# A fused attention and ELU kernel: the hand-fixed order of all five engines replaced by another one

## The chip, the cores and the metric

The kernel runs on one core of a Trainium2 chip. The metric is the time of one execution on the device in microseconds (us). Before the change three runs gave 298.71 us in the median (298.64 to 298.76). A profile was taken of one further execution, which took 298.42 us; its recorded span, from the first to the last instruction of the program, is 296.2 us. Engines are named as in the profile: PE is the matrix engine (PEld its weight loads), DVE the vector engine, ACT the scalar engine, POOL is GpSimd, SP the engine that only issues DMAs here.

## The reference

```python
q_s = exp(q - max(q, -1));  q_s /= sum(q_s, -1)        # softmax over the 64 features
k_s = exp(k - max(k, 2));   k_s /= sum(k_s, 2)         # softmax over the 576 positions
kv  = einsum('bhsd,bhse->bhde', k_s, v)                # batch 8, heads 8, seq 576, dim 64
a   = einsum('bhsd,bhde->bhse', q_s, kv)
x   = a.transpose(0, 2, 1, 3).reshape(4608, 512)
h   = x @ w_in                                         # 512 -> 2048
g   = where(h > 0, h, exp(min(h, 0)) - 1)
out = g @ w_out                                        # 2048 -> 512, float32
```

## The kernel before

**Two pipelines in one.** The attention part works in 16 units n (a batch's four heads each, n = 0 to 15). The feed-forward part works on 9 blocks j of 512 tokens, each in 8 groups g of 256 hidden features. While the feed-forward part works on block j, the attention units that later blocks need are fed in between.

**Attention unit n.** Loads of q, k, v (`load`, L345; on POOL's DMA queue for the early units, on SP's for the later). `stage1`: ACT takes exponentials of q (L380, for units 0 and 1 in halves, L410) and of k (L384); POOL or ACT turns v to bf16 (L400, L397); DVE sums q's exponentials (L412), takes reciprocals (L415); POOL (for units 0 to 3 POOL and DVE) multiplies them in (L423, result QS). QS is transposed on PE (`tp`, L447, copied out by ACT or DVE, L454 and L457) or, from unit 4 on, by a DMA on SP (`turn`, L463) and widened to fp32r by POOL or ACT (`widen`, L473 and L475). PE makes kv (L503), DVE normalizes it (`m`, L512 and L516), PE multiplies by q (L534, L546), and ACT or DVE copies the result to the ring XT (`xt`, L568 and L571).

**Feed-forward block j, group g.** `hg`: eight matmuls of 128x512 (L619) into one of two pairs of PSUM banks; ACT takes exp (L635). From there one of two ways. Way "a": ACT makes relu(1 - e) (L655) and DVE one or two operations max(h, 0) - that (L658). Way "d" (half of the groups of blocks 0 and 1): DVE makes min(e, 1) - 1 in SBUF (L663) and then the max with h (L665). The next matmuls of that bank pair wait for DVE.

**The second product.** For blocks 0 and 1 it is plain (`out_mm`, L680). For later blocks a seven-product scheme for 2x2 blocks of matrices saves matmuls: `pair` (L874, L880) for half of the features, `whole` (L804) for all. It needs differences of blocks of W2 (`combos`, POOL, L739) and, for every token half (ts) and feature half (hi) of a block, four sums of blocks of g (`sums`, L770), on POOL except for the very last set, which DVE makes. DVE and ACT put the parts together (L894, L810, L906, L922, L815), and SP stores (L713).

**What sets the order.** Every call of `S.add` makes one operation: an engine, a modelled duration, the code that emits it, and what it reads and writes. Operations are numbered as they are made, 0 to 1110. The table `ORDER` lists, for each engine, the numbers of its operations in the order in which that engine gets them. `Sched.order` reads this table, gives each operation a modelled start time, and merges the five lists by it; `fill` puts a few warming matmuls on PE in the modelled gaps of the first microseconds (L969); `emit` writes the instructions and a semaphore wait for each input made by another engine or a DMA. On the chip each engine goes through its own list strictly in order: an operation whose input is late holds up all that stand behind it on the same engine. The modelled durations in the kernel are not used for anything else.

Operations that the text names, by number:

| numbers | engine | what |
| --- | --- | --- |
| 14 to 21 | POOL queue | loads of W1: 14 to 17 groups 0 to 2 by quarters, 18, 19, 20 groups 3, 4, 5 (512 KB each), 21 groups 6 and 7 (1 MB) |
| 110, 121, 133 | PE | L619, block 0, groups 5, 6, 7 |
| 163, 224 | POOL queue, ACT | load of q and L380 for unit 5 |
| 225, 226, 227 | DVE, DVE, POOL | L412, L415, L423 for unit 5 |
| 253, 259, 266, 272, 279 | PE | L619, block 1, groups 2 to 6 |
| 254, 255, 256 | ACT, DVE, DVE | L635, L663, L665 of block 1, group 2 |
| 177, 185 | PE, ACT | last quarter of L680 of block 0 for one token tile, and its copy out (L698) |
| 1046, 1047, 1048, 1049, 1050 | PE, ACT, ACT, DVE, DVE | the last group (block 8, group 7): L619, L635, L655, L658 twice; 1042 is the second L658 of group 6 |
| 1063 to 1066 | DVE | L770, the last set of sums, in the order in which they are made |
| 1055 to 1058, 1062 | POOL | L770, the set before it, and the last of another one |
| 1067 to 1107 | PE | L804, the last block's seven-product pieces |
| 1082, 1083, 1085, 1089, 1090 | DVE | L810, putting the last block together |

Of the kernel before, what the change touches and what calls it, by code (L numbers as in the profile page):

```python
# [23 lines left out]
ISSUE = {"sp": 550, "act": 550, "gp": 740}  # L24
ORDER = {
# [14 lines left out]
    "act": (  # L40
# [12 lines left out]
    "dve": (  # L53
# [30 lines left out]
}  # L84


# [1094 lines left out]
```

## Time and profile before

| | |
| --- | --- |
| median of three runs | 298.71 us |
| the profiled execution | 298.42 us, span 296.2 us |
| busy, of the span | PE 284.3 us (96%), ACT 211.3 (71%), POOL 193.3 (65%), DVE 182.2 (62%) |
| chain that ended last | PE 89%, DVE 5%, ACT 3%, DMA 1%, issue 1% |
| DMA | 36.70 MB read, 9.44 MB written |

The page gives, for each engine, busy time and its share of the span, the chain of work that ended last, and groups of instructions by source line with their mean duration and the idle time ahead of them. The list of waits adds up who waited for whom. The timeline shows instructions in order of time: start, length, engine, line, operation, tiles and shapes, and in brackets the idle time ahead of it and what ended it. Since the program's instructions stand in the trace in the order of `ORDER`, each operation's number can be matched to its instruction, and its start and end read off; the landing of a DMA is read from the update of its semaphore.

### The profile page before, as it was taken

How to read it: one execution, taken by the hardware profiler on the slowest of the kernel's cores; microseconds unless marked ns; L12 is line 12 of the kernel's file. 1: busy time of each engine (PE TensorE's matmuls, PEld its weight loads, DVE VectorE, ACT ScalarE, POOL GpSimd, SP SyncE). 2: the span in 40 equal slices, each digit the busy share in tenths (PEclk: the TensorE clock that was granted, in tenths of full speed). 3: DMA queues.
4: the chain of work that ended last, by engine and by line, in shares of the span. 5: the costliest groups of instructions: out<-in, count | busy, mean ns of one | idle time of the engine just before them, and what ended most of it. 6: DMA issues, size and time to landing. Idle time of an engine off the chain costs nothing.

```text
span 296.2 us, 5181 instructions
## 1 busy us (share of the span) xinstructions
PE 284.3 (96%) x2082; PEld 240.9 (81%) x2082; DVE 182.2 (62%) x327; ACT 211.3 (71%) x249; POOL 193.3 (65%) x155
## 2 busy tenths in 40 slices
PE   2999999989999999999999999999999999999984
PEld 0588877678888888888888888888889998988984
DVE  2858645777663858665766575653544645375793
ACT  4868659968998968888967796776564666566610
POOL 1990347615499993849565657368678976859580
PEclk9999999999999999999999999999999999999998
DMA  7999999898794659389398613122020302021205
GB/s 268 398 364 388 389 390 353 236 234 288 210 276 151 161 139 340 69 242 326 85 204 221 218 36 78 40 55 53 18 55 0 73 18 53 20 53 37 62 11 142
DMA packets 36471, 50.01 MB, mean 169 GB/s; under 512 B 16352, under 2 KB 18144, under 8 KB 36448
## 3 DMA queue, kind: packets, MB, share of 16 engines
q1 hardware_dynamic: 29760, 34.09, 41.6%
q0 software_dynamic: 6528, 15.47, 17.1%
q8 instruction: 16, 0.26, 0.4%
q10 hardware_dynamic: 160, 0.13, 0.2%
q14 instruction: 7, 0.06, 0.1%
HBM read 36.70 MB, written 9.44 MB: 156 GB/s over the span
## 4 chain that ended last, share of the span: by engine, by line
PE 89%; DVE 5%; ACT 3%; DMA 1%; issue 1%
PE PS L619 43%; PE PS L804 11%; PE PS L880 10%; PE PS L680 9%; PE PS L874 9%; PE PS L534 3%; PE PS L503 2%; PE PS L969 2%; DMA QR<-in_q_dram 1%; DVE XT L770 1%; ACT ESB L635 1%; DVE GR L658 1%; DVE ESB L663 1%; PE PS L447 1%; DVE GR L665 1%; ACT ESB L655 1%
## 5 line engine op out<-in xcount | busy, mean ns | idle before, releaser
L619 PE MATMUL PS<-XT,W 128*128 128x512 f32 x576 | 142.6, 393 | 1.6 <-DVE GR L665 1.6
L619 PEld LDWEIGHTS PS<-XT,W 128*128 128x128 f32 x576 | 105.2, 188 | 22.8 <-DVE GR L665 1.7
L658 DVE SCALAR_TENSOR_TENSOR GR<-PS,ESB 128x512 fp32r<-128x512 f32 (+1 forms) x124 | 87.3, 706 | 58.4 <-ACT ESB L655 56.7
L635 ACT ACTIVATE ESB<-PS 128x1024 f32<-128x1024 f32 x72 | 73.7, 1026 | 41.0 <-PE PS L619 40.6
L655 ACT ACTIVATE ESB<-ESB 128x1024 f32<-128x1024 f32 x64 | 67.9, 1061 | 1.6
L423 POOL TENSOR_TENSOR QS<-QR,RZQ 128x1152 f16<-128x1152 f32 (+1 forms) x16 | 30.6, 1913 | 37.5 <-DVE RZQ L415 37.3
L770 POOL TENSOR_TENSOR SB<-GR 128x512 fp32r<-128x512 f32 x18 | 23.3, 1296 | 40.7 <-DVE GR L658 20.7
L880 PE MATMUL PS<-W,GR 128*128 128x512 f32 x128 | 33.1, 392 | 0.0
L680 PE MATMUL PS<-W,GR 128*128 128x512 f32 x128 | 32.3, 395 | 0.0
L680 PEld LDWEIGHTS PS<-W,GR 128*128 128x128 f32 x128 | 23.4, 188 | 4.7 <-DVE GR L665 0.2
L880 PEld LDWEIGHTS PS<-W,GR 128*128 128x128 f32 x128 | 22.7, 189 | 3.8
L412 DVE TENSOR_REDUCE ZQ<-QR 128x18 f32<-128x1152 f32 (+2 forms) x18 | 21.8, 1209 | 6.3 <-ACT QR L410 4.4
L770 POOL TENSOR_TENSOR GR<-GR 128x512 fp32r<-128x512 f32 x19 | 25.4, 1343 | 0.0
L770 POOL TENSOR_TENSOR SB<-GR,SB 128x512 fp32r<-128x512 f32 x18 | 23.7, 1314 | 0.6
L770 POOL TENSOR_TENSOR SB<-SB,GR 128x512 fp32r<-128x512 f32 x18 | 23.7, 1316 | 0.5
L568 ACT ACTIVATE XT<-PS 128x512 fp32r<-128x512 f32 (+6 forms) x32 | 19.2, 604 | 6.3 <-PE PS L534 3.0
L400 POOL CAST VB<-VR 128x1152 bf16<-128x1152 f32 (+1 forms) x16 | 17.7, 1108 | 6.3 <-DMA VR<-in_v_dram 6.3
L894 DVE TENSOR_TENSOR OSB<-OSB,PS 128x256 f32<-128x256 f32 x32 | 13.2, 413 | 12.7 <-PE PS L880 6.3
L384 ACT ACTIVATE KR<-KR 128x1152 bf16<-128x1152 f32 x16 | 18.4, 1154 | 0.5 <-DMA KR<-in_k_dram 0.5
L380 ACT ACTIVATE QR<-QR 128x1152 f32<-128x1152 f32 x14 | 16.2, 1159 | 1.3 <-DMA QR<-in_q_dram 1.3
L804 PE MATMUL PS<-W,GR 128*128 128x256 f32 x96 | 14.1, 283 | 0.0
L804 PE MATMUL PS<-TB,GR 128*128 128x256 f32 x96 | 13.5, 285 | 0.6 <-DVE OSB L810 0.6
(80 smaller groups left out, 335.4 us busy)
## 6 DMA issues: line engine op xcount, KB each, us to landing
out_dram<-OSB SPq DMA_DIRECT2D x60, 128.0 KB, 2.4
QR<-in_q_dram SPq DMA_DIRECT2D x12, 576.0 KB, 5.3
KR<-in_k_dram SPq DMA_DIRECT2D x12, 576.0 KB, 5.3
VR<-in_v_dram SPq DMA_DIRECT2D x12, 576.0 KB, 5.5
W<-in_moe_w_out_dram POOLq DMA_DIRECT2D x4, 1024.0 KB, 16.5
QR<-in_q_dram POOLq DMA_DIRECT2D x4, 576.0 KB, 10.9
KR<-in_k_dram POOLq DMA_DIRECT2D x4, 576.0 KB, 11.0
VR<-in_v_dram POOLq DMA_DIRECT2D x4, 576.0 KB, 13.2
```

Source lines behind the costliest of these rows:

```text
L412: S.add("dve", t_dve(m), lambda e, qp=qp, zp=zp: e.tensor_reduce(zp, qp, AX.X, ALU.add), key - 3, R=[f"qR{i}{x}" for x in xs], W=[f"ZQ{i}{ ...
L423: lambda e, qp=q[:, :, a:b, :], rz=rz, dst=qs[:, :, a:b, :]: e.tensor_tensor(dst, qp, rz, ALU.mult),
L568: S.add("act", t_act((h1 - h0) * n_, True), lambda e, dst=dst, src=src: e.activation(dst, src, AF.Copy), key, W=W, X=X)
L619: last = e.matmul(P[:, t * 512:(t + 1) * 512], self.W1[:, kc, tt * 128:(tt + 1) * 128], self.XT[:, kc, rc:rc + BLK], start=(kc == 0), stop ...
L635: S.add("act", t_act(1024, True), lambda e: e.activation(esb[:, :], self.PS[ps][:, :], AF.Exp), key, W=[f"E{i}"], X=banks)
L655: S.add("act", t_act(1024, False), lambda e: e.activation(esb[:, :], esb[:, :], AF.Relu, bias=1.0, scale=-1.0), key, X=[f"E{i}"])
L658: S.add("dve", t_dve(512 if j else 1024), lambda e, u=u: e.scalar_tensor_tensor(*(x[:, :, u, :] if j else x for x in (gt, P)), 0.0, ev[:, ...
L680: last = e.matmul(dst, self.tile(jb, jj, ts), self.W2[:, jj, c0:c1], start=(jj == 0), stop=(jj == 15))
L770: lambda e, dst=dst, a=a, b=b, op=op: e.tensor_tensor(dst, a, b, op), key, R=R, W=W, X=X,
L804: last = e.matmul(dst, a[:, z, :], b[:, z, :], start=start and z == 0, stop=stop and z == NSP - 1, skip_group_check=True)
L874: last = e.matmul(dst, a[:, z, :], b[:, z, :], start=start and z == 0, stop=stop and z == NSP - 1, skip_group_check=True)
L880: last = e.matmul(self.bank((b0, b1)[p]), self.tile(j, jj, 2 * ts + p), self.W2[:, jj, :], start=False, stop=jj == 15, skip_group_check=True)
```

## The change

The table `ORDER` is replaced by another order of the same 1111 operations. The new order was solved for with a model in which VectorE's operations last longer when they run beside GpSimd's. The operations, their code, their durations in the kernel's own model, tiles and buffers are the same; the numbers of the waits and where the merged list puts them follow from the order. Cut to the parts that the text speaks of ("..." marks what is left out):

```diff
     "pe": (
-        "35 54 33 37 52 57 56 60 78 81 64 65 79 82 84 87 85 88 80 83 86 89 99 103 110 121 133 107 "
-        "148 147 150 155 158 156 125 149 157 127 171 145 170 169 151 176 177 153 168 175 159 178 "
-        "172 165 192 194 191 193 253 259 257 258 264 265 211 266 272 270 271 278 220 279 284 222 "
+        "35 54 33 37 52 56 57 60 78 79 82 64 65 81 80 84 87 85 88 83 86 89 99 103 110 121 107 133 "
+        "148 147 149 150 156 125 157 158 127 155 171 168 169 145 175 176 153 151 170 159 178 172 "
+        "165 192 194 191 177 193 253 259 258 257 264 265 211 266 272 220 271 278 270 279 222 277 "
...
-        "1022 953 980 973 990 987 982 1011 998 1003 1031 1017 1067 1006 1026 1043 1024 1038 1034 "
-        "1046 1069 1051 1070 1072 1071 1073 1068 1077 1075 1088 1081 1084 1079 1095 1091 1098 "
+        "1022 953 973 980 987 982 990 1003 998 1011 1031 1017 1006 1026 1024 1043 1038 1034 1046 "
+        "1067 1051 1070 1069 1072 1068 1073 1071 1077 1075 1081 1084 1079 1088 1095 1091 1098 "
         "1103 1107 "),
     "act": (
...
-        "109 135 115 126 137 146 152 182 138 185 154 179 198 173 166 188 224 249 250 195 207 199 "
-        "254 260 261 210 297 267 273 274 221 280 223 230 286 232 287 236 293 294 233 308 348 240 "
+        "135 115 109 126 137 146 138 182 152 154 179 198 173 166 188 224 249 250 185 195 199 207 "
+        "254 260 261 210 297 267 273 274 221 233 280 223 230 286 232 287 236 293 294 348 308 334 "
...
     "dve": (
...
-        "225 226 251 252 196 197 255 256 262 263 212 213 214 215 216 217 268 269 275 276 298 299 "
+        "225 251 252 196 197 255 226 256 262 263 212 213 214 215 216 217 268 269 275 276 298 281 "
...
-        "1001 1002 1032 1033 1020 1007 1021 1029 1030 1035 1044 1045 1041 1042 1052 1049 1050 "
-        "1063 1064 1065 1089 1066 1082 1083 1085 1090 1096 1097 1092 1099 1100 1104 1108 "),
+        "1001 1002 1032 1033 1020 1021 1029 1030 1007 1044 1035 1045 1041 1052 1049 1050 1042 "
+        "1063 1064 1082 1083 1066 1065 1085 1089 1090 1096 1097 1092 1099 1100 1104 1108 "),
     "gp": (
-        "1 32 48 14 15 24 16 17 18 40 19 20 21 68 69 70 71 72 74 73 75 76 77 120 131 116 144 143 "
-        "163 132 139 164 200 205 203 208 227 234 300 237 386 303 311 318 387 388 390 314 321 391 "
+        "1 32 48 14 15 24 17 16 18 40 19 21 20 68 69 70 71 72 73 74 75 76 77 120 116 131 144 143 "
+        "163 139 164 132 200 205 203 208 227 234 300 237 386 303 311 318 387 388 390 391 314 321 "
...
-        "867 873 896 874 897 898 915 916 917 899 969 972 970 971 962 963 964 965 918 994 997 995 "
-        "1013 1059 1060 1014 996 1061 1015 1016 1055 1056 1057 1058 1062 "),
+        "866 896 873 897 874 898 915 916 917 969 899 970 971 918 962 963 965 964 994 995 972 996 "
+        "1013 1016 997 1059 1060 1014 1061 1015 1062 1055 1056 1057 1058 "),
     "sp": (
-        "8 9 10 11 12 13 184 186 190 204 206 209 189 180 228 183 219 218 235 181 229 187 301 238 "
+        "8 9 10 11 12 13 180 204 206 187 183 209 218 181 228 229 219 184 186 235 189 190 301 302 "
...
```

72 rows, old and new, of the table ORDER are left out of this document.

## The prediction

> **What bounds the kernel now.** I read the page's first part and its chain first, then the waits of PE alone, then the timeline at the two places where those waits fall.
>
> ```profile
> span 296.2 us, 5181 instructions
> PE 284.3 (96%) x2082; PEld 240.9 (81%) x2082; DVE 182.2 (62%) x327; ACT 211.3 (71%) x249; POOL 193.3 (65%) x155
> PE 89%; DVE 5%; ACT 3%; DMA 1%; issue 1%
> ...
> PE PS L969 <- ACT QR L410: 5.5, 1, 5.5
> PE PS L619 <- DVE GR L665: 1.6, 1, 1.6
> PE PS L804 <- DVE OSB L810: 0.6, 1, 0.6
> PE PS L804 <- DVE XT L770: 0.3, 1, 0.3
> ```
>
> PE is the bound; the change moves its work but takes none away. A new order can win only where PE waits, and the four waits are all that the profile shows. The first is the first load. The other three, 2.5 us, are all for DVE. So the case has little to win, and anything to lose. The two places:
>
> ```profile
> 53.95 0.68 DVE L663 TENSOR_SCALAR ESB<-ESB 128x1024 f32<-128x1024 f32 x1
> ...
> 56.38 2.12 POOL L423 TENSOR_TENSOR QS<-QR,RZQ 128x1152 f16<-128x1152 f32 x1
> 56.99 2.06 DVE L663 TENSOR_SCALAR ESB<-ESB 128x1024 f32<-128x1024 f32 x1 [1.09 <-ACT ESB L635]
> 59.09 1.22 DVE L665 TENSOR_TENSOR GR<-ESB,PS 128x1024 fp32r<-128x1024 f32 x1
> 60.36 0.50 PE L619 MATMUL PS<-XT,W 128*128 128x512 f32 x1 [1.60 <-DVE GR L665]
> ```
>
> The same L663 takes 0.68 us alone and 2.06 beside POOL's L423. It ends at 59.05, 0.55 us after POOL's operation (58.50): it did its own work only after that. PE waits 1.60 us for what follows.
>
> ```profile
> 280.49 1.16 DVE L770 TENSOR_TENSOR XT<-GR 128x512 fp32r<-128x512 f32 x1
> 281.69 1.66 DVE L770 TENSOR_TENSOR XT<-XT,GR 128x512 fp32r<-128x512 f32 x1
> 283.39 1.66 DVE L770 TENSOR_TENSOR XT<-GR,XT 128x512 fp32r<-128x512 f32 x1
> 285.30 1.45 DVE L770 TENSOR_TENSOR GR<-GR 128x512 fp32r<-128x512 f32 x1
> ...
> 279.81 1.30 POOL L770 TENSOR_TENSOR SB<-GR 128x512 fp32r<-128x512 f32 x1 [2.90 <-DVE GR L658]
> 281.19 1.62 POOL L770 TENSOR_TENSOR SB<-SB,GR 128x512 fp32r<-128x512 f32 x1
> 282.88 1.61 POOL L770 TENSOR_TENSOR SB<-GR,SB 128x512 fp32r<-128x512 f32 x1
> 284.46 3.42 POOL L770 TENSOR_TENSOR GR<-GR 128x512 fp32r<-128x512 f32 x2
> ...
> 283.40 1.22 PE L804 MATMUL PS<-TB,XT 128*128 128x256 f32 x8 [0.33 <-DVE XT L770]
> 287.58 1.22 PE L804 MATMUL PS<-TB,GR 128*128 128x256 f32 x8 [0.57 <-DVE OSB L810]
> ```
>
> The last sums run on DVE and POOL at once and take turns: each DVE operation ends about 0.55 us after a POOL one (281.65 after 281.11, 283.35 after 282.81, 285.05 after 284.50). DVE's four take 5.9 us, and the L810 that PE needs stand behind them.
>
> **The change part by part**, each on the clock of the profiled execution.
>
> *The L663 at 57 us: -1.0.* In DVE's new list 226 (L415, 0.27 us), which releases POOL's 227, stands behind 255. So 227 cannot run beside it: 255 takes 0.68, then 226 0.27, then 256 1.22. Against that, ACT reaches 254 later: 185 (0.59) now stands ahead of 195. From the q of unit 5, which landed at 49.1, ACT does 224, 249, 250 (1.06 each), 185 (0.5), 195, 199, 207 (1.06 each): 254 starts at about 56.0, before 55.93. Then 1.03 + 0.68 + 0.27 + 1.22 and four handovers of 0.04 give 59.35 for 266, where it was 60.36. PE's own work would bring it there at 59.0 to 59.2, so the most is -1.3; the least is 0, if that load lands 1 us later; more than that is left out, since the loads ahead of it in POOL's queue are the same and the stores beside it are fewer. 227 ends at 60.2 instead of 58.5; SP's transpose 228 waits for it (60.1 before, 61.0 now) and its result is first read at 69.15.
>
> *The loads of W1: 0.* On POOL's queue 21 (1 MB) goes ahead of 20. These loads land in the order of issue: 18 at 18.46, 19 at 19.99, 20 at 21.87, 21 2.70 later. So 20 lands at 24.56, and PE's 110, which began at 24.04, waits some 0.55. Behind it PE meets loads that have not moved (W2's third quarter at 38.7, its last at 41.43, the v of unit 3 at 44.40) and then the wait for 256, which hangs on ACT's chain; these take up the 0.55. If they did not: +0.55. Quarter 17 ahead of 16 costs nothing, since PE asks for 16 at 17.2 and it lands at 16.2. Copy 55 behind 59 puts 79 at 14.95; by group 3 PE stands at 20.5 against 20.41.
>
> *Unit 6's k ahead at 67 us: +0.2.* ACT does 233 (1.1 us) ahead of 280, 223, 230 and 232. PE's 231 needs 230, which then ends about 0.2 us after PE is free. Between 0 and +0.4.
>
> *The end: -1.15.* PE takes 1067 (0.48 us) behind 1046 instead of ahead of 1026, so 1046 and all that hangs on it (1047 to 1050) come 0.48 earlier: 1050 ends at 279.98. 1042 (0.69) now follows, and 1063 begins at 280.68. POOL has done 1062 ahead of 1055 in a stretch where it sat idle 2.9 us. DVE's 1063 and 1064 still take turns with POOL's 1056 and 1057 and end by 282.95 (284.25 if POOL goes first). But now 1082 and 1083 come next, as soon as PE's 1081 is done: they end at 284.9 instead of 287.53. 1066 and 1065 run last, after POOL's last sum (285.4), at 0.6 each, to 286.6; then 1085, 1089, 1090 (0.42 each) to 287.9. PE's pieces of 0.96 and 0.48 from 282.92 run on with a gap of 0.2 ahead of 1084 (1057 ends at 284.1) and reach 1107, released by DVE's 1100, at 290.05 instead of 291.21. The most is -1.6 (no gap at all); if POOL's row ahead of 1055 slips by its 1.1 us of slack and as much again, 0.
>
> *All the rest: 0.* I laid PE's new list out with each operation's own cadence in this trace and set against it the ends of its inputs, those that now stand behind another one on ACT, DVE or POOL moved by that one's length. Some forty places come close; by hand they all fit. The tightest are 457 at 105 us (380 now stands behind 447 and 412: no slack), 741 at 187 us (723 behind 666 and 738: 0.1) and 1043 at 271 us (997 behind 1013 and 1016: 0.45). Loads that fall back on SP, such as the q of unit 13 behind a store (issued near 144 instead of 134.8, read at 152.9), still land in time. What I missed can only cost: 0 to +0.8.
>
> The sum is -1.0 + 0 + 0.2 - 1.15 = -1.95: 298.42 becomes 296.47. That execution stood 0.29 under the median of the runs, so the median comes to 296.76, or 296.8. The ends of the terms (-1.3, 0, 0, -1.6, 0 and 0, 0.55, 0.4, 0, 0.8) allow 295.8 to 300.5.
>
> **The rivals.**
>
> *Part of the gain at 57 us is lost to a POOL cast.* The next L663, 268, moves 1 us forward to 62.55. POOL's cast of unit 6's v (L400, 1.15 us) starts when that load lands, 62.2 before. If the cast comes first and blocks as L423 did, 268 ends at 63.35 + 0.55 = 63.9 instead of 63.25, 269 at 65.1, and PE's 279, due at 64.8, waits 0.3: 297.1. No row shows an L663 beside a cast. [...] In the new order two stores are issued ahead of that load, which speaks for a later landing and no clash.
>
> *The gain at 57 us does not come.* 254 hangs on one row of ACT operations; if it starts 1 us later, 266 is where it was, and only the end wins: 297.8.
>
> *The end wins nothing.* POOL's nine sums from 266.7 on (1.28 each) reach 1055 only 1.1 us ahead of its data, and 997 is 0.45 ahead of PE's need; if they slip, only the start wins: 297.9.
>
> *Slower: DVE's list blocks itself.* The new list puts DVE operations that wait for PE ahead of ones that free PE's banks: 128 ahead of 136, 447 ahead of 380, 666 and 738 ahead of 723, 890 and 891 ahead of 858, 1004 ahead of 985. PE then waits for its own earlier piece plus 0.7 us of L658. Where PE arrives early this costs up to 0.7 per place; three such places eat the gain, from the fourth on it is over 0.6 us slower, and all five with the W1 wait give 298.71 - 1.95 + 3.5 + 0.55 = 300.8; 299.6 for four (298.71 - 1.95 + 2.8). Against it: in each I found the producer's end at or ahead of PE's need.
>
> **How the numbers follow.** A difference under 0.2%, 0.6 us, is about what a measurement of this kernel cannot tell from none. The forecast (by itself 296.2 to 297.3) has 0.47, the clash with the cast 0.11; only the end 0.10; only the start 0.06; gains eaten to within 0.6 us of before 0.10; slower 0.16. So faster 0.74, the same 0.10, slower 0.16. The range reaches from 295.9, the most at both places less 0.1, to 298.9, which leaves out the slower cases and little else.
>
> **What would show it.** Right: all L663 under 0.8 us, POOL's L423 of unit 5 after 58 us, PE's wait there 0.4 us or less; at the end 13.7 us from the end of PE's last L619 to the start of its last piece 1107, where it was 14.4 (276.85 to 291.21) without the 0.48 of 1067, and DVE's last L770 at 0.6 us. A new wait of PE for POOL's W1 load of about 0.5 us near 24 us that does not show in the end. Wrong: any new wait of PE for DVE or ACT over 0.3 us between 65 and 275 us, above all at 457, 741 and 1043; or the L658 of block 1 no earlier than before.

## The result and the profile after

The changed kernel takes 296.50 us (median of 7 runs, 296.28 to 297.73), the kernel before 298.64 us in the runs beside it (median of 7). The ratio is 0.9936, with a 95% interval of 0.9906 to 0.9965: faster by 0.6%, 2.1 us. The profiled execution took 296.28 us.

The first part of the changed kernel's page, and its chain:

```profile
span 294.5 us, 5191 instructions
PE 283.3 (96%) x2082; PEld 240.4 (82%) x2082; DVE 179.0 (61%) x327; ACT 210.2 (71%) x249; POOL 193.1 (66%) x155
PE 85%; DMA 5%; ACT 4%; POOL 3%; DVE 1%; POOLq 1%; issue 0%; SPq 0%
```

DVE is busy for 3.2 us less with the same 327 instructions, and its share of the chain fell from 5% to 1%. PE's waits (waited for, us in total, times, longest):

```profile
PE PS L969 <- ACT QR L410: 5.5, 1, 5.5
PE PS L619 <- DMA W<-in_moe_w_in_dram: 0.9, 1, 0.9
PE PS L503 <- POOL VB L400: 0.3, 1, 0.3
PE PS L804 <- POOL SB L770: 0.3, 1, 0.3
PE PS L447 <- DVE QS L423: 0.2, 1, 0.2
```

The three waits for DVE (1.6, 0.6 and 0.3 us) are gone. New are 0.9 us for a load of W1, twice 0.3 us for results of POOL, and 0.2 us for a product that DVE makes. The place near 57 us in the timeline (start, length, engine, line, operation; in brackets the idle time ahead and what ended it):

```profile
56.16 1.15 POOL L400 CAST VB<-VR 128x1152 bf16<-128x1152 f32 x1 [3.23 <-DMA VR<-in_v_dram]
57.36 0.70 DVE L663 TENSOR_SCALAR ESB<-ESB 128x1024 f32<-128x1024 f32 x1 [1.09 <-ACT ESB L635]
57.97 0.26 DVE L415 RECIPROCAL RZQ<-ZQ 128x18 f32<-128x18 f32 x1
58.15 1.17 DVE L665 TENSOR_TENSOR GR<-ESB,PS 128x1024 fp32r<-128x1024 f32 x1
58.31 2.12 POOL L423 TENSOR_TENSOR QS<-QR,RZQ 128x1152 f16<-128x1152 f32 x1 [1.00 <-DVE RZQ L415]
59.68 1.67 PE L619 MATMUL PS<-XT,W 128*128 128x512 f32 x6
```

The L663 (255) takes 0.70 us where it took 2.06, since POOL's L423 comes after it. PE's 266 starts at 59.68 without a wait. Over the whole kernel the eight L663 now lie close together (shortest, median, longest in ns; before 630/684/2065):

```profile
L663 DVE TENSOR_SCALAR ESB<-ESB x8: 681/694/696, 19.1 to 68.5; 128x1024 f32<-128x1024 f32 x8
```

The end, in the same view:

```profile
279.89 0.69 DVE L770 TENSOR_TENSOR XT<-GR 128x512 fp32r<-128x512 f32 x1
280.62 1.67 DVE L770 TENSOR_TENSOR XT<-XT,GR 128x512 fp32r<-128x512 f32 x1
283.36 0.88 DVE L810 TENSOR_TENSOR OSB<-OSB,PS 128x256 f32<-128x256 f32 x2 [1.08 <-PE PS L804]
284.15 1.07 DVE L770 TENSOR_TENSOR GR<-GR 128x512 fp32r<-128x512 f32 x1
285.15 0.68 DVE L770 TENSOR_TENSOR XT<-GR,XT 128x512 fp32r<-128x512 f32 x1
...
281.81 1.62 POOL L770 TENSOR_TENSOR SB<-GR,SB 128x512 fp32r<-128x512 f32 x1
283.39 1.29 POOL L770 TENSOR_TENSOR GR<-GR 128x512 fp32r<-128x512 f32 x1
...
283.57 0.71 PE L804 MATMUL PS<-W,SB 128*128 128x256 f32 x4 [0.25 <-POOL SB L770]
```

DVE's four sums take 4.1 us instead of 5.9, and the two L810 that PE needs run between them, not behind them. What is late next is a sum of POOL (1057): PE waits 0.25 us for it.

The start of one PE operation against that in the kernel before says where the time went. PE comes to 253 at 53.29 us, 1.23 later than before; at 266 it is 0.68 ahead, at 292 (71.8 us) 0.57, at 953 (253.05 us) 0.71, at 1107 (289.57 us) 1.64. So in this execution some 0.7 us come from the place at 57 us, next to nothing from the 180 us between, and 0.93 from the end. That is 1.64 us at 1107; the executions differ by 2.14, and part of what is left lies outside the recorded span (see the table of experiments).

### The profile page after: what moved, and what is told of

The parts are those of the page before. It is cut to its first block, busy times and chain, and to the rows that moved or that the text cites. A ratio compares the mean times of both kernels' runs of the same rounds, so it can differ in the third digit from the quotient of the medians.

```text
span 294.5 us, 5191 instructions
## 1 busy us (share of the span) xinstructions
PE 283.3 (96%) x2082; PEld 240.4 (82%) x2082; DVE 179.0 (61%) x327; ACT 210.2 (71%) x249; POOL 193.1 (66%) x155
## 4 chain that ended last, share of the span: by engine, by line
PE 85%; DMA 5%; ACT 4%; POOL 3%; DVE 1%; POOLq 1%; issue 0%; SPq 0%
PE PS L619 41%; PE PS L804 11%; PE PS L880 10%; PE PS L874 9%; PE PS L680 9%; DMA W<-in_moe_w_in_dram 3%; PE PS L534 3%; DMA QR<-in_q_dram 2%; PE PS L503 2%; POOL W L361 1%; POOL SB L770 1%; ACT ESB L655 1%; ACT QR L380 1%; ACT ESB L635 1%; POOLq L271 1%; POOL VB L400 1%
## 5 line engine op out<-in xcount | busy, mean ns | idle before, releaser
L619 PE MATMUL PS<-XT,W 128*128 128x512 f32 x576 | 143.0, 393 | 0.9 <-DMA W<-in_moe_w_in_dram 0.9
L619 PEld LDWEIGHTS PS<-XT,W 128*128 128x128 f32 x576 | 105.3, 188 | 22.7 <-DMA W<-in_moe_w_in_dram 1.3
L655 ACT ACTIVATE ESB<-ESB 128x1024 f32<-128x1024 f32 x64 | 68.0, 1062 | 1.5
L423 POOL TENSOR_TENSOR QS<-QR,RZQ 128x1152 f16<-128x1152 f32 (+1 forms) x16 | 30.9, 1934 | 38.9 <-DVE RZQ L415 38.8
L770 POOL TENSOR_TENSOR GR<-GR 128x512 fp32r<-128x512 f32 x19 | 24.7, 1301 | 0.0
L400 POOL CAST VB<-VR 128x1152 bf16<-128x1152 f32 (+1 forms) x16 | 17.7, 1109 | 7.7 <-DMA VR<-in_v_dram 7.7
L473 POOL CAST qsT<-QT 128x1152 fp32r<-128x1152 f16 x10 | 11.5, 1148 | 16.5 <-PE PS L534 9.5
L894 DVE TENSOR_TENSOR OSB<-OSB,PS 128x256 f32<-128x256 f32 x32 | 13.3, 415 | 12.8 <-PE PS L880 5.3
L810 DVE TENSOR_TENSOR OSB<-OSB,PS 128x256 f32<-128x256 f32 x23 | 9.5, 418 | 12.5 <-PE PS L804 10.6
```

Source lines behind the costliest of these rows:

```text
L400: lambda e, dst=dst, src=src: e.tensor_copy(dst, src), key - 50,
L423: lambda e, qp=q[:, :, a:b, :], rz=rz, dst=qs[:, :, a:b, :]: e.tensor_tensor(dst, qp, rz, ALU.mult),
L619: last = e.matmul(P[:, t * 512:(t + 1) * 512], self.W1[:, kc, tt * 128:(tt + 1) * 128], self.XT[:, kc, rc:rc + BLK], start=(kc == 0), stop ...
L655: S.add("act", t_act(1024, False), lambda e: e.activation(esb[:, :], esb[:, :], AF.Relu, bias=1.0, scale=-1.0), key, X=[f"E{i}"])
L770: lambda e, dst=dst, a=a, b=b, op=op: e.tensor_tensor(dst, a, b, op), key, R=R, W=W, X=X,
```

## The experiments

Each kernel is the one before or the changed one with some numbers of `ORDER` moved. In their profiles the line numbers are lower by one (L662 is L663). The kernel before, run beside them, had medians of 298.45 us (the first four kernels), 298.51 (the next four) and 298.51 (the last four); a ratio to them is uncertain by 0.14 to 0.28%. The start of a PE operation differs from one profiled execution to another: 253 stands at 52.03, 52.69 and 52.97 us in three kernels whose orders are the same up to there. A distance between two starts near the end is far sharper: from 953 to 1107 PE took 37.45 to 37.47 us in the four profiles with the whole old end, and 36.52 or 36.53 in the eight with the whole new one. "Outside" is what an execution takes beyond its recorded span (mean).

| kernel | 255 takes | 266 starts | 1107 starts | 953 to 1107 | median us | outside |
| --- | --- | --- | --- | --- | --- | --- |
| before | 2.06 | 60.36 | 291.21 | 37.45 | 298.45 to 298.64 | 2.23 |
| changed | 0.70 | 59.68 | 289.57 | 36.52 | 296.50 | 1.81 |
| changed, once more | 0.70 | 59.86 | 289.84 | 36.52 | 296.59 | 1.79 |
| before, 226 later | 0.69 | 58.95 | 290.35 | 37.46 | 297.63 | 2.22 |
| before, new end | 2.08 | 60.46 | 290.45 | 36.53 | 297.12 | 1.79 |
| before, both | 0.69 | 59.59 | 289.56 | 36.52 | 296.26 | 1.79 |
| before, 1067 later | 2.08 | 60.54 | 291.03 | 37.06 | 298.08 | 2.24 |
| before, new end, 1062 last | 1.80 | 60.08 | 290.76 | 37.24 | 297.64 | 1.80 |
| before, both, 209 later | 0.69 | 59.89 | 289.84 | 36.52 | 296.04 | 1.82 |
| before, new order of W1 | 1.76 | 60.63 | 291.54 | 37.47 | 298.85 | 2.23 |
| changed, old order of W1 | 0.69 | 59.63 | 289.55 | 36.52 | 296.26 | 1.83 |
| changed, W1 and 132 as before | 0.69 | 60.09 | 289.98 | 36.52 | 295.86 | 1.79 |
| changed, 226 back | 1.94 | 61.45 | 292.93 | 36.53 | 298.22 | 1.81 |
| changed, old end | 0.69 | 60.56 | 291.65 | 37.46 | 297.70 | 1.79 |

The last column holds something that no start of an instruction shows. Every execution of the kernel before and of the three with 2.22 to 2.24 that has its span on record (114 in all) spends 2.18 to 2.30 us outside its span, and each of the 88 executions of the others 1.74 to 1.87. The profiles of the two sets also differ in the count of instructions (5181, against 5182 or more) and in a line of the page's DMA queues (queue, kind: packets, MB, share); here of the kernel before and of the changed one:

```profile
q14 instruction: 7, 0.06, 0.1%
q14 instruction: 8, 0.07, 0.1%
```

All four kernels with 2.2 us have 7 packets, all others 8. So some 0.44 us of a difference between the two sets come with the program, whatever its engines do, and not with one execution; what in the program brings them was not tried.

### The reciprocal alone

```diff
 "dve"
-225 226 251 252 196 197 255 256
+225 251 252 196 197 255 226 256
```

> The kernel before with one edit: on DVE the reciprocal 226 (L415), which releases POOL's 227 (L423), stands behind 255 (L663) instead of ahead of 251. Theory (POOL's L423 held 255 up): no L663 is over 0.8 us, 255 ends some 1.3 us earlier, 266 starts at about 59.3 us (60.36 before), PE's wait there falls from 1.60 to 0.6 us or less, and what was won is kept to the end: 1107 starts at about 290.2 (291.21), time 297.4 to 297.9. Rival one (something other than that lock keeps 266 where it was, such as PE's own 211): 266 within 0.2 us of 60.36, time unchanged. Rival two (won at 57 us, lost again behind it): 266 early, 1107 within 0.3 us of 291.2.

Measured: 297.63 us, 0.8 us under the kernel before; the ratio of 0.9981 (0.9961 to 1.0001) only just reaches 1, so here the trace carries the verdict. 255 takes 0.69 us, 266 starts at 58.95, 1.41 us earlier. Of this, 0.86 is left at 1107. The loss is soon behind 266:

```profile
61.77 1.15 POOL L399 CAST VB<-VR 128x1152 bf16<-128x1152 f32 x1 [1.75 <-DMA VR<-in_v_dram]
62.16 1.30 DVE L662 TENSOR_SCALAR ESB<-ESB 128x1024 f32<-128x1024 f32 x1 [0.22 <-ACT ESB L634]
...
64.77 2.14 PE L618 MATMUL PS<-XT,W 128*128 128x512 f32 x8 [0.18 <-DVE GR L664]
```

This is the prediction's first rival, in another kernel than the one it was made for: POOL's cast of unit 6's v begins first, 268 takes 1.30 us and ends 0.54 us after the cast, and the matmuls of 279 start 0.34 us later than their cadence would have it. So both readings hold in part: the theory at 57 us, and a third of a microsecond lost again to the next operation of POOL.

### The end alone, and parts of it

The kernel before, with the changed kernel's lists from 953 (PE), 946 (DVE) and the matching places of the other engines on; the core of it:

```diff
 "pe"
-1031 1017 1067 1006 1026 1043 1024 1038 1034 1046 1069 1051 ... 1075 1088 1081 1084 1079 1095
+1031 1017 1006 1026 1024 1043 1038 1034 1046 1067 1051 ... 1075 1081 1084 1079 1088 1095
 "dve"
-1041 1042 1052 1049 1050 1063 1064 1065 1089 1066 1082 1083 1085 1090
+1041 1052 1049 1050 1042 1063 1064 1082 1083 1066 1065 1085 1089 1090
 "gp"
-1061 1015 1016 1055 1056 1057 1058 1062
+1061 1015 1062 1055 1056 1057 1058
```

> The kernel before up to some 255 us, with the end of the changed kernel's order on all five engines from there (PE behind 953, DVE behind 946, ACT, POOL and SP at matching places). Theory (the gain at the end is worth what was forecast and does not hang on the rest): L663 at 57 us still 2.06 us and PE's wait there still 1.6 us; at the end DVE's last L770 about 0.7 us, 1107 starts at about 290.1 to 290.25 (291.21 before), time 297.3 to 297.7. Rival (the gain at the end came only because PE arrived earlier, or the last sums are bounded by POOL): 1107 at 290.9 or later, time within 0.3 us of before.

Measured: 297.12 us (ratio 0.9965, 0.9944 to 0.9985). The wait at 57 us is as it was (1.63 us), and from 953 to 1107 PE takes 36.53 us instead of 37.45: 0.92 less. The gain at the end does not hang on the rest. Of the 1.33 us by which the median is lower, the 0.44 outside the span are the other part.

Only 1067 moved behind 1046 on PE:

```diff
 "pe"
-1017 1067 1006 1026 1043 1024 1038 1034 1046 1069
+1017 1006 1026 1043 1024 1038 1034 1046 1067 1069
```

> The kernel before with one edit: PE takes 1067 behind 1046 instead of ahead of 1026. Theory: 1046 starts 0.48 us earlier, the last sums of DVE and POOL all move by 0.48 and still take turns (DVE's four last 5.9 us in all), PE's waits of 0.33 and 0.57 us at the end shrink to 0 and 0.4, and 1107 starts at 291.21 - 0.48 = 290.7. So half of the gain at the end is the place of 1067 and half the order of the sums on DVE and POOL. Rival (the place of 1067 is nothing by itself, since the sums wait for something else): 1107 within 0.1 us of 291.2. Rival (it is all of the gain): 1107 at 290.3.

Measured: 298.08 us (ratio 0.9978, 0.9960 to 0.9997); 37.06 us from 953 to 1107, 0.39 less than before. PE's two waits there:

```profile
283.23 1.22 PE L803 MATMUL PS<-TB,XT 128*128 128x256 f32 x8
287.41 1.21 PE L803 MATMUL PS<-TB,GR 128*128 128x256 f32 x8 [0.56 <-DVE OSB L809]
```

The first (0.33) is gone, the second stands at 0.56. DVE's four sums still take 5.9 us. So 0.39 us of the end are 1067's, and the other 0.53 come from the rest of the new end, of which the next run takes out one part.

The new end, but with 1062 last on POOL:

```diff
 "gp"
-1061 1015 1062 1055 1056 1057 1058
+1061 1015 1055 1056 1057 1058 1062
```

> The kernel before with the changed kernel's end, but with POOL's 1062 last again, behind 1058. Theory (DVE's L770 takes turns with POOL's as long as POOL has one to do): 1065, DVE's last L770, starts beside 1062 and ends about 0.55 us after it, some 0.7 us later than with 1062 moved; the L810 behind it move with it, and 1107 starts 0.3 to 0.7 us later than in the run with the whole new end (290.45 there). Rival (1062's place is nothing, since the DVE operations behind 1083 have slack): 1107 within 0.15 us of 290.45.

Measured: 297.64 us (ratio 0.9975, 0.9961 to 0.9989); 37.24 us from 953 to 1107, 0.71 more than with the whole new end.

```profile
283.86 2.99 POOL L769 TENSOR_TENSOR GR<-GR 128x512 fp32r<-128x512 f32 x2
...
285.62 1.78 DVE L769 TENSOR_TENSOR XT<-GR,XT 128x512 fp32r<-128x512 f32 x1
...
288.57 3.40 PE L803 MATMUL PS<-TB,GR 128*128 128x256 f32 x24 [0.37 <-DVE OSB L809]
```

POOL's last sum ends at 286.85, DVE's at 287.40, 0.55 later, and PE waits 0.37 us for the L810 behind it. Without 1062's early place the rest of the new end gains nothing over 1067 alone: 37.24 us against 37.06. (That the median is 0.44 us under that run's, 297.64 against 298.08, is the time outside the span.)

### The changed kernel with one part undone

```diff
 "dve"
-225 251 252 196 197 255 226 256
+225 226 251 252 196 197 255 256
```

> The changed kernel with one edit: on DVE the reciprocal 226 stands directly behind 225 again, ahead of 251, so that POOL's 227 (L423) can run as soon as the cast 208 ends (57.31 in the changed kernel, where 255 began at 57.36). Theory (POOL's L423 holds 255 up): L423 starts at about 57.3, 255 takes 2 us or more and ends 0.55 us after it, near 60.0; 266 starts near 61.2 instead of 59.68, and the time is 1.0 to 1.5 us over the changed kernel's. If instead 255 gets in a few hundredths of a microsecond ahead of L423, 255 takes 0.7 us and nothing is lost. Rival (the place of 226 is not what the changed kernel's gain at 57 us hangs on): 255 at 0.7 us with L423 running since well before it, time unchanged.

Measured: 298.22 us (median of 12), 1.6 over the changed kernel run beside it (296.59).

```profile
57.47 2.12 POOL L422 TENSOR_TENSOR QS<-QR,RZQ 128x1152 f16<-128x1152 f32 x1
58.19 1.94 DVE L662 TENSOR_SCALAR ESB<-ESB 128x1024 f32<-128x1024 f32 x1 [1.83 <-ACT ESB L634]
...
61.45 1.44 PE L618 MATMUL PS<-XT,W 128*128 128x512 f32 x4 [1.70 <-DVE GR L664]
```

255 ends at 60.14, 0.55 us after POOL's operation, and 266 starts at 61.45. This one number's place is worth more here than in the kernel before (0.8 us). In the new order POOL's 227 begins 1.1 us later (57.47 against 56.38), and in the kernel before a third of a microsecond was lost again to the cast; the two were not told apart. Against the kernel before, this one is not faster (ratio 1.0004, 0.9984 to 1.0025), though it has the whole new end: in its profile PE comes to 266 1.09 us later than in that kernel. (The profiled execution took 299.64 us; why it stands over the median is told under the hardware below.)

The old end on all five engines, from the same places as above:

> The changed kernel with the end of the kernel before on all five engines from some 255 us on. Theory (the end is worth what it was worth alone): the waits of 0.33 and 0.57 us and DVE's L770 of 1.45 to 1.67 us are back, 1107 starts 0.9 to 1.0 us later than in the changed kernel, near 290.5, and the time is 0.8 to 1.2 us over the changed kernel's. Rival (in the changed kernel the end gains only by arriving earlier): within 0.3 us of the changed kernel.

Measured: 297.70 us, 1.1 over the changed kernel; 37.46 us from 953 to 1107, exactly the old end's. In this execution the wait for W1 was 1.4 us and unit 4's k landed at 55.37 us (53.52 in the changed kernel's profile); PE is 0.88 later at 266 than there, and 1107 is later than in the kernel before.

### Both edits, nothing else

The kernel before with 226 behind 255, and the new end:

> The kernel before with both small edits: 226 behind 255 on DVE, and the changed kernel's order from some 255 us on. Theory (the two gains add up, and the rest of the new order is worth nothing): 1107 starts at 291.21 - 0.86 - 0.92 = 289.4 us (289.57 in the changed kernel), time 296.4 to 296.9. As in the run with the first edit alone, 268 (L663, near 62 us) runs beside POOL's cast and takes about 1.3 us. Rival (the gains overlap, since the end hangs on something that does not move with PE): 1107 at 290.0 or later. Rival (the rest of the new order brings something too): 1107 clearly behind the changed kernel's, 289.9 or later.

Measured: 296.26 us (ratio 0.9931, 0.9903 to 0.9958), the changed kernel's time within the uncertainty, and 1107 at 289.56 against 289.57. The time outside the span is the changed kernel's too. So with 226 behind 255, the rest of the new order, on all five engines from 12 to 250 us, is worth nothing that can be measured. The expected clash of 268 with the cast did not happen: PE was 0.6 us later at 266 than with the first edit alone, 268 began at 62.82, 0.15 us ahead of the cast's end, and took 0.69 us.

With the load of unit 6's v (209) put behind the transpose 228 on SP:

```diff
 "sp"
-204 206 209 189 180 228 183
+204 206 189 180 228 209 183
```

> The run before this one with one more edit: on SP's queue the load of unit 6's v (209) stands behind the transpose 228, so that POOL's cast of it (L400) starts some 3 us later, clear of 268. Theory (the cast holds that L663 up, as POOL's L423 held 255 up): 268 takes 0.69 us instead of 1.30 and ends near 62.9, PE's wait of 0.3 us at 279 goes, and 1107 starts 0.3 to 0.5 us earlier, at 288.9 to 289.1; time 0.3 to 0.5 us lower. Rival (268 is slow for another reason, or PE's own work keeps 279): 279 and 1107 where they were, within 0.1 us. Rival (the later load is missed at the kv product of unit 6 near 75 us): a new wait of PE there.

Measured: 296.04 us (ratio 0.9911, 0.9883 to 0.9939). POOL's cast now runs at 68.08 and 268 takes 0.69 us, but it did so without this edit too, and PE lost 0.3 us to a load of W2 near 42 us in this execution. The moved cast met another L663, begun at 68.90: it takes 0.88 us and ends 0.55 after the cast. The run does not tell the theory from its first rival. No new wait at unit 6's kv product appeared.

### The loads of W1, and what takes up their wait

The kernel before with the changed kernel's order of these loads, and the changed kernel with the order of before:

```diff
 "gp"
-15 24 16 17 18 40 19 20 21 68
+15 24 17 16 18 40 19 21 20 68
```

> The kernel before with one edit: the loads of W1 on POOL's queue in the changed kernel's order (17 ahead of 16, 21 ahead of 20). Theory (absorbed): PE waits 0.5 to 0.9 us for 20 near 24 us, PE's place at 253 is late by as much or less, but 266 still starts at 60.3 to 60.5 since it waits for DVE, and the time is within 0.2 us of before. Rival (passed through): 266 at 60.9 to 61.2, time 0.5 to 0.9 us over before.

> The changed kernel with one edit: the loads of W1 on POOL's queue in the order of before (16 ahead of 17, 20 ahead of 21). PE's wait of 0.86 us for 20 near 24 us must go; the question is how much of it reaches 266. Theory (what follows absorbs it: 266 hangs on DVE's 255 and 256 by 59.3 us): 266 starts at 59.3 to 59.5 instead of 59.68, and the time is 0.2 to 0.4 us under the changed kernel's. Rival (the wait was passed through whole): 266 at 58.9 or earlier, time 0.8 us or more under the changed kernel's. Rival (PE loses it to other waits ahead of 253): 266 unchanged, time unchanged. In 255's place: the cast 208 on POOL ended 0.05 us ahead of 255 in the changed kernel; if 255 starts earlier beside it, a longer L663 would show that a cast blocks it as L423 did.

Measured: put into the kernel before, the order makes PE wait 0.69 us and be late by 0.61 at 253, 0.27 at 266 and 0.33 at 1107; 298.85 us against 298.45 (ratio 1.0020, 0.9998 to 1.0042). About half of it is passed through, as far as single executions tell: 266 stands at 60.08 to 60.54 in the four other profiles in which 226 and the first half are as before. Taken out of the changed kernel, the wait goes, PE is 0.59 earlier at 253, and the gain is gone at 266 (59.63 against 59.68); 296.26 us against 296.50, no difference. The reason expected for this was not the right one. ACT, in the timeline of that kernel:

```profile
54.46 2.22 ACT L383 ACTIVATE KR<-KR 128x1152 bf16<-128x1152 f32 x2 [0.67 <-DMA KR<-in_k_dram]
```

The new order of POOL's queue also has unit 5's k (164) ahead of unit 4's (132), which ACT needs first. 132 lands at 54.44 (50.89 before), ACT waits 0.67 us, and 254, 255 and 256 are late behind it. In the changed kernel run once more ACT waits 0.57 us for it.

So the next kernel has both put back:

```diff
 "gp"
-17 16 18 40 19 21 20 ... 163 139 164 132 200 205
+16 17 18 40 19 20 21 ... 163 132 139 164 200 205
```

> The changed kernel with the loads of W1 in the order of before, and besides with the load of unit 4's k (132) ahead of unit 5's (164) on POOL's queue as in before; with W1 alone ACT had waited 0.67 us for 132, which landed at 54.44. Theory (that load took the place of the wait for W1): 132 lands at about 51, ACT starts 254 at 55.8 to 56.0 instead of 56.6, 266 starts at 59.0 to 59.2 instead of 59.63, and the time falls by 0.3 to 0.6 us below the changed kernel's. From there 268 may meet POOL's cast of unit 6's v (61.4 to 62.5) and end at 63.1 instead of 63.5, at no cost to PE or at 0.3 us. Rival (266 hangs on DVE or on PE's own work there): 266 at 59.5 or later, time unchanged.

Measured: 295.86 us (6 runs; ratio 0.9915, 0.9889 to 0.9942), the lowest median of all, but not to be told from the changed kernel's (0.9944, 0.9925 to 0.9962, in the third set). 132 lands at 50.09 and ACT no longer waits for it, yet 254 starts at 57.03 and 266 at 60.09, against what the theory had. The loads behind 132 moved up with it:

```profile
54.05 1.15 POOL L399 CAST VB<-VR 128x1152 bf16<-128x1152 f32 x1 [1.19 <-DMA VR<-in_v_dram]
54.09 1.65 DVE L662 TENSOR_SCALAR ESB<-ESB 128x1024 f32<-128x1024 f32 x1 [0.20 <-ACT ESB L634]
```

Unit 5's v lands at 53.99 instead of 55.8, POOL's cast begins 0.04 us ahead of an L663 (196, block 1's first group), and that L663 ends 0.54 us after the cast, 1 us late. In this profile the wait has moved twice: from W1 to unit 4's k, and from there to a cast. The profiled execution took 296.69 us, the longest of the six; why the median is low is not explained by it.

### The changed kernel once more

> The changed kernel once more, on the chip of the three runs before this one, to see what of its first half is the order and what is one execution's landings. Theory: no L663 that starts clear of a POOL operation is over 0.7 us; if a load lands otherwise and POOL's cast 208 or 234 runs when 255 or 268 starts, that L663 ends some 0.55 us after the cast. PE's wait for W1's 20 is 0.5 to 0.9 us again, 266 starts between 59.3 and 60.2, 1107 between 289.2 and 290.0, time 296.1 to 296.7. Rival (the landings are the same each time): every start within 0.1 us of the first profile, but for the length of the first wait.

Measured: 296.59 us (6 runs). The wait for W1 is 0.8 us, all L663 take 0.7 us, 266 starts at 59.86 and 1107 at 289.84. The landings do differ: ACT's wait for 132 is 0.57 us here and none in the first profile, and PE waits 0.26 us for 256 here.

## Why the prediction was right, step by step

**In sum.** Forecast 296.8, measured 296.50. From the profiled execution before to the one after, the trace gives 1.64 us at 1107 where the terms summed to 1.95; the executions themselves differ by 2.14 us (298.42 to 296.28). 0.44 us of that lie outside the recorded span (2.22 us of the execution before, 1.78 of the one after), which no term reckoned with. So the two places and the mechanisms were right, and that the number came so near is partly luck: the terms brought 0.31 us less than forecast, and a part that nobody had reckoned with made up for it.

**The L663 at 57 us: -1.0 forecast, -0.68 and -0.50 in the two profiles of the changed kernel, -0.86 alone, 1.6 lost when it is undone.** The mechanism was right: in all six profiles in which L423 began ahead of 255, 255 took 1.76 to 2.08 us, in the eight others 0.69 to 0.70. The size was off in one step: the working took 1.0 from DVE's chain (59.35) and had PE's own work there at 59.0 to 59.2. But PE came 1.23 us late to 253, from the W1 wait and delays of up to 0.2 behind it, and its own last work ahead of 266 ended at 59.7. DVE's chain had ended at 59.32, as forecast, but by two errors that cancel: 254 began at 56.30 where the working had 56.0, and from the start of 255 to the end of 256 it took 1.96 us where the working had 2.25, since 226 and 256 each begin some 0.1 us before the one ahead of them ends. With the edit alone PE was not late, and 266 started at 58.95, beyond the forecast's most. There 0.34 went to the cast.

**The loads of W1: 0 forecast, 0 measured in the changed kernel, +0.33 in the old order.** The wait was 0.7 to 0.9 us in four executions and 1.4 in a fifth, not 0.55; in the changed kernel's profile 20 landed at 24.73 (24.56 forecast), and PE came 0.28 us sooner. The loads named as taking it up did not: PE is late by more at 253 than the wait itself. At 266 it is worth 0.33 us at most (59.68, where DVE's chain would have let it start at 59.35), and in the run without it ACT's later row took that. The working had looked at what stands ahead of 163 in POOL's queue, not at the exchange of 132 and 164 behind it.

**Unit 6's k: +0.2 forecast, 0.1 at most.** PE's lead falls from 0.68 at 266 to 0.57 at 292, which takes in 231 and all else there; no wait for 230 shows.

**The end: -1.15 forecast, -0.93 measured.** The undersized term is the gap ahead of 1084: 0.2 forecast, 0.41 measured between starts (0.25 of it idle), since POOL's 1057 ended 0.3 us after PE was there. 1067 was taken at 0.48 and measured 0.39. From the end of PE's last L619 to 1107 it is 13.91 us (13.7 forecast). That POOL's 1062 runs early was in the working, and its run put 0.71 us on it.

**All the rest: 0 forecast, 0 measured.** PE's lead is 0.57 at 292 and 0.71 at 953, no wait over 0.2 us stands between 65 and 275 us, and the kernel with the two edits alone is as fast as the changed one. This holds with 226 behind 255; with 226 back, the kernel with the rest of the new order is no faster than the one before. The places named as tightest (457, 741, 1043) held.

**The rivals.** The clash with the cast did not come in the changed kernel: 268 started at 62.91, the cast had ended at 62.77. The reason given against it, a later landing, did not hold: that load landed at 61.57 us where it was 62.18 before, and the cast was over because it began early. It came in the kernel with 226 alone, at the price given for it (0.3 us), and at another L663 in the kernel with W1 and unit 4's k put back. That the start or the end would win nothing is answered by the changed kernel's own profile (255 at 0.70 us, 36.52 from 953 to 1107) and by the two runs with one part alone in the kernel before. No place showed DVE's list blocking itself.

**The rule behind it.** In nine profiles an L663 began 0.3 us or more before the end of a POOL operation, and each time it ended 0.54 to 0.55 us after it: behind L423 six times, behind the cast L400 three times. Two that began 0.15 and 0.10 us before a cast's end took their usual 0.69. The other way round, an L423 near 69 us that began 0.12 to 0.29 us into an L663 took 2.44 to 2.57 us in eight profiles; one of the same shape beside other operations of DVE takes 2.11 to 2.13. So in these profiles, but for those two, it was the one begun second that took longer, beside a cast too, of which the trace of before had no row.

## What to carry to other kernels

Of a new order for 1111 operations three things were shown to be worth their time: one small operation of 0.27 us that released a POOL operation at the wrong moment, one PE operation that could wait behind the last group's matmuls, and one POOL operation that could run where POOL was idle, together with the order of the sums around it. They can be found by looking for one line whose instructions have the same shape and unlike lengths, and for what PE waits. Where several loads and engines stand within half a microsecond of each other, taking one wait away brings the next one forward (W1, then a load of k, then a cast), so the gain is to be priced at the second latest of what an operation needs, and PE's own work is one of them.

## What the runs showed of the hardware that was not expected

After one long wait of PE another 1.6 us were lost at a lower clock. In the profiled execution of the changed kernel with 226 back, PE had idled 1.70 us ahead of 266, after 0.78 us of small 64x64 matmuls. The stretches behind it (start and end, length, busy time of PE, PEld, DVE, ACT and POOL with the count of instructions, then granted clock, DMA share, GB/s):

```profile
62.00:63.00 1.00, 1.00 (x4) 0.83 (x3) 0.94 (x3) 0.27 (x1) 1.00 (x1) 0.60 0.79 302
63.00:64.00 1.00, 1.00 (x4) 0.71 (x4) 0.86 (x5) 0.00 (x0) 0.13 (x1) 0.50 1.38 335
64.00:65.00 1.00, 1.00 (x4) 0.81 (x3) 0.29 (x1) 0.37 (x1) 0.00 (x0) 0.50 2.04 81
65.00:66.00 1.00, 1.00 (x5) 0.78 (x4) 0.31 (x1) 0.66 (x1) 0.00 (x0) 0.69 0.30 68
66.00:67.00 1.00, 1.00 (x7) 0.82 (x5) 0.97 (x2) 0.00 (x0) 0.00 (x0) 1.00 1.24 300
```

From about 62.2 to 65.6 us the granted clock is 0.5, the matmuls of 128x512 follow each other at 0.43 us instead of 0.23, and eight of them lose 1.6 us. Three of this kernel's 12 executions had a mean granted clock of 0.994 and took 299.64 to 300.02 us; the other nine took 297.81 to 299.05. Of the kernel before, whose wait at this place is 1.6 us, 8 of 80 executions had 0.991 to 0.993 and took 300.25 to 300.87 us; one more has 0.948 on record at 298.48 us, not longer than the others, and is not explained. Of 12 with the new end alone (a wait of 1.63 us) one had 0.994, of 32 with waits of 1.3 to 1.6 us none had less than 0.997, and of the 66 executions of kernels in which 255 was not held up none had less than 0.996. So the executions at 0.991 to 0.994 are some 2 us longer, which no median shows, and all of them belong to kernels whose profile has a wait of 1.60 us or more there. That the idle time sets the clock off is read from these counts and from one trace, and was not tried by itself.
